# Moving eight folds out of the last unit of a spectral mixing stage, behind a stream of weights

## The chip, the cores and the metric

The kernel runs on one core of one Trainium2 chip. The metric is the device time of one execution in microseconds (us), the median of several runs. The profile is of one execution; its span, from the first to the last instruction, is a little shorter than that execution's time.

## The reference, cut to what matters

```python
# attention with a forgetting gate: q, k, v are (8, 8, 576, 64), f is (8, 8, 576)
log_f = np.log(np.clip(f, 0.0001, 1.0)); cum = np.cumsum(log_f, axis=-1)
scores = scale * q @ k^T + cum[..., :, None] - cum[..., None, :]     # causal
attn_out = softmax(scores) @ v
x = attn_out.transpose(0, 2, 1, 3).reshape(8, 576, 512)

# spectral mixing: w_r, w_i are (64, 512, 512), w_ch is (512, 512), all float32
X = np.fft.rfft(x, axis=1)
Xr, Xi = (np.real(X[:, :n_modes]), np.imag(X[:, :n_modes]))
Yr = np.einsum('bmd,mde->bme', Xr, w_r) - np.einsum('bmd,mde->bme', Xi, w_i)
Yi = np.einsum('bmd,mde->bme', Xr, w_i) + np.einsum('bmd,mde->bme', Xi, w_r)
Y[:, :n_modes] = Yr + 1j * Yi                                         # 64 modes
u = x + np.fft.irfft(Y, n=S, axis=1)
return (u + np.maximum(u @ w_ch, 0.0)).astype(np.float32)             # (8, 576, 512)
```

## The kernel before, in words

The kernel has three stretches. First comes the attention, in 32 steps of two heads each, which leaves x in SBUF (`x_all`, bf16). During it, and after it, the mode weights stream in from memory. Then comes the mixing proper, and last the output stage. The instructions of every engine are issued in the order in which the program is written.

**Units and tiles.** The 64 modes are taken in 16 *units* of 4 modes (`u` from 0 to 15). The weights of a unit come in four *tiles* (`dc` from 0 to 3), each 1 MB in bf16, called (u, dc) here. Tiles with `dc` 0 and 1 hold a quarter of the rows of both `w_r` and `w_i`; tile (u, 2) holds half of the rows of `w_r` and tile (u, 3) the same half of `w_i`. All tiles of `dc` 0 and the first twelve of `dc` 1 are used during the attention. The loop over `u` after it takes the others: tiles 2 and 3 of units 0 to 11, and tiles 1, 2 and 3 of units 12 to 15.

**The stream.** `issue_w` starts the transfer of the next tile in a fixed list (`wseq`), on GpSimd's queue, in one or two DMAs (L156, L165); the last tile, (15, 3), comes in four pieces. Buffers come from a pool of seven (`wpool`), so that a transfer waits for the products of the tile seven before it, and by the semaphores also for the landing of the eighth transfer before it. The call of `issue_w` stands behind the products of each tile.

**The products.** `spec_mms` multiplies a tile with the spectrum of x into a PSUM tile `A` (L194, 8 products of 512 columns). After a unit's last tile, `Yb` is the sum of `A` and what the attention stage had left (VectorE, L744), and four small products with a permutation turn it (L747). The result goes to `YT` for units 0 to 11 (the first 48 modes), and to `YL` for units 12 to 15 (L758). The last unit has its products the other way round (`spec_cols`, L211, 32 products of 16 columns a tile), summed in `accT`.

**The folds.** `xw(b)` computes x times `w_ch` for batch element `b`, in units 2 to 10. A *fold* adds the first 48 modes of one batch element to `x_all` and to that product (`XW`). `fold_modes(b)` turns `YT` (L673) and multiplies it with `w_ch` (L684); ScalarE copies both out of PSUM (L681, L692). `fold` then takes five blocks of rows: the old `x_all` by an identity product (L702), the modes times the inverse basis (L705), a copy back into `x_all` by ScalarE (L706), the modes of the product (L710), and an addition into `XW` by VectorE (L711). This is 8 + 15 = 23 matrix products for each batch element.

Before the change, unit 12 + n takes the folds of batch elements 2n and 2n + 1, ahead of the products of its tiles 1 and 2. So folds 6 and 7 are in unit 15; of fold 7 two blocks of rows stand ahead of the products of tile (15, 2), and three behind them.

**The output stage.** `bases(0)` puts `x_all` and `XW` of the first output block into PSUM (L785); then come the products of tile (15, 3), the last sums into `YL` (L839), the last 16 modes turned (L812) and multiplied with `w_ch` (L823), and for each of 20 blocks the bases, the last modes (L800), a copy by ScalarE (L854), the ReLU and sum by VectorE (L855), and the store (L860, L865).

Of the kernel before, what the change touches and what calls it, by code (L numbers as in the profile page):

```python
# [23 lines left out]
def kernel(  # L24
# [12 lines left out]
    B, H, S, Dh = q.shape  # L37
# [4 lines left out]
    NSB = 5  # L42
    SBLK = [128, 128, 128, 128, 64]
    NEB = D // 128
    BH = B * H
    NPAIR = B * H // 2
    NU = NM // 4
    NF = 12
# [131 lines left out]
    def spec_mms(A, u, dc, first, last):  # L180
        w8 = wtile.pop((u, dc))
        for n in range(2):
            for j in range(4):
                m = 4 * u + j
                st_, sp_ = first and n == 0, last and n == 1
                if dc < 2:
                    M = 32
                    c0 = m * 24 + (8 if n == 0 else 0)
                    lhsT, rhs = XS[:, dc, c0 : c0 + 32], w8[:, n, j, :]
                else:  # L190
                    M = 32 if st_ else 16
                    c0 = 24 * n + (8 if dc == 2 else 0)
                    lhsT, rhs = XPv[:, c0 : c0 + M, m], w8[:, j, n, :]
                nc.tensor.matmul(  # L194
                    A[32 * j : 32 * j + M, :], lhsT=lhsT, rhs=rhs, start=st_, stop=sp_
                )
# [426 lines left out]
    with ExitStack() as bctx:  # L623
# [8 lines left out]
        with ExitStack() as mctx:  # L632
            xtp = mctx.enter_context(tc.tile_pool(name="xtp", bufs=1))
            fsb = mctx.enter_context(tc.tile_pool(name="fsb", bufs=2))
            psA = mctx.enter_context(tc.tile_pool(name="psA", bufs=2, space=PSUM))
            psT = mctx.enter_context(tc.tile_pool(name="psT", bufs=2, space=PSUM))
            psX = mctx.enter_context(tc.tile_pool(name="psX", bufs=4, space=PSUM))

            def xw(b):

                xT = xtp.tile([128, NEB, S], BF16, tag="xT", name="xT")
                for eb in range(NEB):
                    ptr = psT.tile([128, S], BF16, tag="t", name="ptr")
                    for sc in range(NSB):
                        ns = SBLK[sc]
                        nc.tensor.transpose(
                            ptr[:, sc * 128 : sc * 128 + ns],
                            x_all[:ns, eb, b, sc, :],
                            ident_bf[:ns, :ns],
                        )  # L650
                    nc.vector.tensor_copy(xT[:, eb, :], ptr[:, :])  # L651
                if b < 3:
                    XW[b] = xw2.tile([128, NSB, D], BF16, tag="xw", name="XW")
                else:
                    XW[b] = yx[:, b - 3, :].bitcast(BF16).rearrange("p (s e) -> p s e", s=NSB)
                for sb in range(NSB):
                    Ms = SBLK[sb]
                    pxw = psX.tile([128, D], F32, tag="x", name="pxw")
                    for eb in range(NEB):
                        nc.tensor.matmul(  # L660
                            pxw[:Ms, :],
                            lhsT=xT[:, eb, sb * 128 : sb * 128 + Ms],
                            rhs=wch[:, eb, :],
                            start=(eb == 0),
                            stop=(eb == NEB - 1),
                        )
                    nc.scalar.copy(XW[b][:Ms, sb, :], pxw[:Ms, :])  # L667

            def fold_modes(b):

                py = psX.tile([128, D], F32, tag="x", name="py")
                for eb in range(NEB):
                    nc.tensor.matmul(  # L673
                        py[:KF, eb * 128 : (eb + 1) * 128],
                        lhsT=YT[:, eb, b, 0:KF],
                        rhs=ident_bf[:, :],
                        start=True,
                        stop=True,
                    )
                y_sb = fsb.tile([128, D], BF16, tag="ysb", name="y_sb")  # L680
                nc.scalar.copy(y_sb[:KF, :], py[:KF, :])  # L681
                pyw = psX.tile([128, D], F32, tag="x", name="pyw")
                for eb in range(NEB):
                    nc.tensor.matmul(  # L684
                        pyw[:KF, :],
                        lhsT=YT[:, eb, b, 0:KF],
                        rhs=wch[:, eb, :],
                        start=(eb == 0),
                        stop=(eb == NEB - 1),
                    )  # L690
                yw_sb = fsb.tile([128, D], BF16, tag="ywsb", name="yw_sb")
                nc.scalar.copy(yw_sb[:KF, :], pyw[:KF, :])  # L692
                return y_sb, yw_sb

            def fold(b, ys, sbs):

                y_sb, yw_sb = ys
                for sb in sbs:
                    Ms = SBLK[sb]
                    bi = BI[:KF, sb * 128 : sb * 128 + Ms]  # L700
                    pu = psX.tile([128, D], F32, tag="x", name="pu")
                    nc.tensor.matmul(  # L702
                        pu[:Ms, :], lhsT=ident_bf[:Ms, :Ms], rhs=x_all[:Ms, :, b, sb, :], start=True, stop=False
                    )
                    nc.tensor.matmul(pu[:Ms, :], lhsT=bi, rhs=y_sb[:KF, :], start=False, stop=True)  # L705
                    nc.scalar.copy(  # L706
                        x_all[:Ms, :, b, sb, :], pu[:Ms, :].rearrange("p (g c) -> p g c", g=NEB)
                    )
                    pz = psX.tile([128, D], F32, tag="x", name="pz")
                    nc.tensor.matmul(pz[:Ms, :], lhsT=bi, rhs=yw_sb[:KF, :], start=True, stop=True)  # L710
                    nc.vector.tensor_tensor(  # L711
                        XW[b][:Ms, sb, :], pz[:Ms, :], XW[b][:Ms, sb, :], ALU.add
                    )

            xw_plan = {2: 0, 3: 1, 5: 2, 6: 3, 7: 4, 8: 5, 9: 6, 10: 7}
            for u in range(NU):
                last = u == NU - 1
                if not last:
                    A = psA.tile([128, D], F32, tag="a", name="A1")
                first = 2 if u < NX else 1  # L720
                for dc in range(first, NEB - 1 if last else NEB):
                    if dc == NEB - 1 and u in xw_plan:
                        xw(xw_plan[u])
                    split = NSB
                    if u >= NF and dc < 3:
                        b = 2 * (u - NF) + dc - 1
                        split = 2 if b == B - 1 else NSB
                        ys = fold_modes(b)
                        fold(b, ys, range(split))
                    if last:  # L730
                        AT = psA.tile([128, NEB, 8, B], F32, tag="a", name="AT1")
                        spec_cols(AT, dc)
                        nc.vector.tensor_tensor(
                            accT[:], AT[:].rearrange("p e c b -> p e b c"), accT[:], ALU.add
                        )
                    else:
                        spec_mms(A, u, dc, dc == first, dc == NEB - 1)
                    issue_w()
                    if split < NSB:
                        fold(b, ys, range(split, NSB))  # L740
                if last:
                    break
                Yb = ybpool.tile([128, D], BF16, tag="yb", name="Yb")
                nc.vector.tensor_tensor(Yb[:], A[:], yacc[u // 2][:, u % 2, :], ALU.add)  # L744
                yps = psT.tile([128, NEB, 64], F32, tag="t", name="yps")
                for eb in range(NEB):
                    nc.tensor.matmul(  # L747
                        yps[:, eb, :],
                        lhsT=Yb[:, eb * 128 : (eb + 1) * 128],
                        rhs=perm[:],  # L750
                        start=True,
                        stop=True,
                    )
                if u < NF:
                    ydst = YT[:, :, :, 8 * u : 8 * u + 8]
                else:
                    ydst = YL[:, :, :, 8 * (u - NF) : 8 * (u - NF) + 8]
                nc.vector.tensor_copy(  # L758
                    ydst,
                    yps[:].rearrange("p eb (b c) -> p eb b c", b=8),  # L760
                )
# [134 lines left out]
```

## Time and profile before

| what | value |
|---|---|
| median of 3 runs | 442.66 us (439.27 to 443.81) |
| the profiled execution: its own time | 442.7 us |
| the profiled execution: span | 440.7 us |
| mean granted TensorE clock | 0.936 |
| PE busy | 344.5 us, 78% of the span |
| DVE busy | 268.4 us, 61% |
| ACT busy | 233.3 us, 53% |
| GpSimd's DMA queue | 85.64 MB, at 104.9% of 16 engines' span |
| chain that ended last: transfers / PE / DVE | 39% / 34% / 19% |

PE is TensorE's matrix products, PEld its weight loads, DVE VectorE, ACT ScalarE, POOL GpSimd. In a row of the order of time stand the start, the length, the engine, the line, the operation, the tile written and the tiles read, how many, and in brackets the idle time before it with what ended it. A granted clock of 1.00 is TensorE's full clock, and 0.50 half of it.

### The profile page before, as it was taken

How to read it: one execution, taken by the hardware profiler on the slowest of the kernel's cores; microseconds unless marked ns; L12 is line 12 of the kernel's file. 1: busy time of each engine (PE TensorE's matmuls, PEld its weight loads, DVE VectorE, ACT ScalarE, POOL GpSimd, SP SyncE). 2: the span in 40 equal slices, each digit the busy share in tenths (PEclk: the TensorE clock that was granted, in tenths of full speed). 3: DMA queues.
4: the chain of work that ended last, by engine and by line, in shares of the span. 5: the costliest groups of instructions: out<-in, count | busy, mean ns of one | idle time of the engine just before them, and what ended most of it. 6: DMA issues, size and time to landing. Idle time of an engine off the chain costs nothing.

```text
span 440.7 us, 10287 instructions
## 1 busy us (share of the span) xinstructions
PE 344.5 (78%) x4295; PEld 189.9 (43%) x4305; DVE 268.4 (61%) x641; ACT 233.3 (53%) x355; POOL 129.7 (29%) x199
## 2 busy tenths in 40 slices
PE   1678878889889889898893694797885788979993
PEld 0455555555555565555551241343442233325331
DVE  6678888777887778888871221223231356635885
ACT  4567678778787665665640031132222355734673
POOL 6544444453454444444222111012211221100000
PEclk9999999999999999999997598599989699969997
DMA  8999999999999999999999999999999999992698
GB/s 190 205 234 221 230 220 231 232 228 227 231 231 222 231 222 229 221 230 224 232 212 212 212 212 212 212 212 212 211 212 210 211 210 210 210 210 53 219 347 294
DMA packets 68349, 96.75 MB, mean 220 GB/s; under 512 B 3536, under 2 KB 45008, under 8 KB 68304
## 3 DMA queue, kind: packets, MB, share of 16 engines
q0 software_dynamic: 62800, 85.64, 104.9%
q1 hardware_dynamic: 5504, 10.47, 6.8%
q8 instruction: 33, 0.54, 0.4%
q14 instruction: 12, 0.10, 0.1%
HBM read 163.73 MB, written 9.44 MB: 393 GB/s over the span
## 4 chain that ended last, share of the span: by engine, by line
DMA 39%; PE 34%; DVE 19%; ACT 3%; issue 3%; POOL 1%; DVEq 0%; POOLq 0%; ACTq 0%
DMA w<-in_moe_w_i_dram 22%; DMA w<-in_moe_w_r_dram 15%; DVE vT L384 5%; DVE x_all L492 4%; DVE qkT L360 4%; PE pav L477 4%; PE A L194 4%; PE sps L432 3%; PE tv L382 3%; PE pd L521 3%; PE vp L393 2%; PE U L785 2%; DMA qk<-in_k_dram 2%; PE Z L785 2%; DVE vn L372 2%
## 5 line engine op out<-in xcount | busy, mean ns | idle before, releaser
L439 ACT ACTIVATE et<-sps 128x1024 bf16<-128x1024 f32 x96 | 96.0, 1050 | 12.6 <-PE sps L432 10.2
L744 DVE TENSOR_TENSOR Yb<-A,yx 128x512 bf16<-128x512 f32 x15 | 10.4, 692 | 67.6 <-PE A L194 67.6
L477 PE MATMUL pav<-vs,et 128*128 128x65 bf16 (+1 forms) x896 | 51.2, 197 | 0.2 <-DVE vn L372 0.2
L360 DVE COPY qkT<-tp 128x640 bf16<-128x640 bf16 x64 | 48.8, 763 | 3.1 <-PE tp L355 3.0
L477 PEld LDWEIGHTS <-et 128*128 128x128 bf16 (+1 forms) x896 | 36.5, 102 | 17.2 <-issue 13.3
L194 PE MATMUL A<-w,XP 128*16 128x512 bf16 (+1 forms) x240 | 22.6, 457 | 27.1 <-DMA w<-in_moe_w_i_dram 15.6
L660 PE MATMUL pxw<-wch,xT 128*128 128x512 bf16 (+1 forms) x152 | 39.1, 403 | 1.0 <-DVE xT L651 0.4
L432 PE MATMUL sps<-qkT 64*128 64x512 bf16 (+4 forms) x320 | 38.9, 306 | 1.1 <-DVE qkT L360 1.1
L492 DVE TENSOR_TENSOR x_all<-pav,rcp 128x384 bf16<-128x384 f32 (+2 forms) x96 | 36.2, 377 | 3.3
L355 PE MATMUL tp<-ident_bf,qk 128*64 128x128 bf16 x576 | 29.3, 231 | 9.9 <-DMA qk<-in_k_dram 9.9
L384 DVE COPY vT<-tv 128x576 bf16<-128x576 bf16 x32 | 24.2, 757 | 19.3 <-PE tv L382 19.3
L667 ACT CAST XW<-pxw 128x512 bf16<-128x512 f32 (+1 forms) x15 | 8.8, 585 | 48.3 <-PE pxw L660 48.3
L165 POOL DMA_DIRECT2D w<-in_moe_w_r_dram x16 | 11.9, 743 | 70.1 <-PE A L194 56.7
L404 ACT COPY vs<-vp 128x576 bf16<-128x576 bf16 x32 | 20.5, 640 | 21.4 <-PE vp L400 21.4
L156 POOL DMA_DIRECT2D w<-in_moe_w_r_dram x27 | 20.5, 759 | 38.5 <-PE A L194 8.6
L667 ACT CAST yx<-pxw 128x512 bf16<-128x512 f32 (+1 forms) x25 | 14.6, 585 | 32.4 <-PE pxw L660 32.4
L165 POOL DMA_DIRECT2D w<-in_moe_w_i_dram x19 | 13.3, 700 | 55.8 <-PE A L194 26.1
L109 POOL DMA_DIRECT2D qk<-in_q_dram x32 | 19.7, 614 | 33.8 <-PE tp L355 7.8
L706 ACT CAST x_all<-pu 128x512 bf16<-128x512 f32 (+1 forms) x40 | 23.4, 584 | 9.0 <-PE pu L705 8.0
L491 DVE RECIPROCAL rcp<-pav 128x6 f32<-128x6 f32 (+2 forms) x96 | 16.2, 169 | 16.3 <-PE pav L477 16.1
L156 POOL DMA_DIRECT2D w<-in_moe_w_i_dram x27 | 20.4, 756 | 17.5 <-DMA w<-in_moe_w_i_dram 8.2
L109 POOL DMA_DIRECT2D qk<-in_k_dram x32 | 19.4, 605 | 20.2 <-DMA w<-in_moe_w_r_dram 6.5
(134 smaller groups left out, 666.5 us busy)
## 6 DMA issues: line engine op xcount, KB each, us to landing
w<-in_moe_w_r_dram POOLq DMA_DIRECT2D x16, 1024.0 KB, 29.6
w<-in_moe_w_i_dram POOLq DMA_DIRECT2D x15, 1024.0 KB, 32.1
w<-in_moe_w_r_dram POOLq DMA_DIRECT2D x27, 512.0 KB, 11.1
w<-in_moe_w_i_dram POOLq DMA_DIRECT2D x27, 512.0 KB, 12.5
vt<-in_v_dram POOLq DMA_DIRECT2D x29, 288.0 KB, 10.6
out_dram<-o_sb SPq DMA_DIRECT2D x16, 512.0 KB, 3.4
qk<-in_q_dram POOLq DMA_DIRECT2D x32, 144.0 KB, 10.7
qk<-in_k_dram POOLq DMA_DIRECT2D x32, 144.0 KB, 10.8
```

The costliest lines, as they stand in the source:

```text
L109: nc.gpsimd.dma_start(qk[64 * n : 64 * n + 64, :, :], src[b, 2 * g : 2 * g + 2, :, :].rearrange("h (p r) d -> p h (r d)", p=64),)
L156: nc.gpsimd.dma_start(w8[:, t, :, :], src[4 * u : 4 * u + 4, dc * 128 : (dc + 1) * 128, :].rearrange("m p e -> p m e"),)
L165: nc.gpsimd.dma_start(w8[:, j : j + step, :, :].rearrange("p m r e -> p m (r e)"), src[m : m + step, 256:512, :].rearrange("m (p r) e -> p ...
L194: nc.tensor.matmul(A[32 * j : 32 * j + M, :], lhsT=lhsT, rhs=rhs, start=st_, stop=sp_)
L355: nc.tensor.transpose(tp[64 * hp : 64 * hp + 64, r - r0, :, :].rearrange("p n c -> p (n c)"), qk[:, hp, r * 64 : r * 64 + 64], ident_bf[:, :],
L360: nc.vector.tensor_copy(st[i]["T"][:].rearrange("p n (c r) -> p n c r", r=9)[:, :, :, r0:r1], tp[:, 0 : r1 - r0, :, :].rearrange("p r n c ...
L384: nc.vector.tensor_copy(st[i]["vT"][:].rearrange("p (c r) -> p c r", r=9), tv[:].rearrange("p r c -> p c r"))
L432: nc.tensor.matmul(ps[:, hp, c : c + n], lhsT=KT[sl, jb * 128 : jb * 128 + 128], rhs=QT[sl, i0 : i0 + n], start=True, stop=True,)
L439: nc.scalar.activation(st[i]["et"][:, T, :, :], ps[:], ACT.Exp, scale=scale)
L477: nc.tensor.matmul(pav[:Ms, sb % 3, hp, :], lhsT=eblk(i, hp, jb, sb), rhs=rhs, start=(jb == 0), stop=(jb == sb),)
L492: nc.vector.tensor_tensor(x_all[:ns, g, b, lo:hi, :].rearrange("p s (h d) -> p s h d", h=2), pav[:ns, lo % 3 : lo % 3 + n, :, 0:Dh], _stri ...
L660: nc.tensor.matmul(pxw[:Ms, :], lhsT=xT[:, eb, sb * 128 : sb * 128 + Ms], rhs=wch[:, eb, :], start=(eb == 0), stop=(eb == NEB - 1),)
```

## The change

The eight folds are taken in units 12 to 14, three to a unit, in the order of the batch elements. The first two of a unit stand ahead of the products of its tiles 1 and 2, as before. The third stands behind the products of its tile 3, after the sum into `Yb` and ahead of the four small products with the permutation. Unit 14 takes only two, ahead of its tiles 1 and 2, and the last unit none. A fold is no longer split.

```diff
-            def fold(b, ys, sbs):
+            def fold(b, ys):
 
                 y_sb, yw_sb = ys
-                for sb in sbs:
+                for sb in range(NSB):
...
             xw_plan = {2: 0, 3: 1, 5: 2, 6: 3, 7: 4, 8: 5, 9: 6, 10: 7}
+            steps = [(u, dc) for u in range(NF, NU - 1) for dc in range(1, NEB)]
+            fold_plan = dict(zip(steps, range(B)))
             for u in range(NU):
...
-                    split = NSB
-                    if u >= NF and dc < 3:
-                        b = 2 * (u - NF) + dc - 1
-                        split = 2 if b == B - 1 else NSB
-                        ys = fold_modes(b)
-                        fold(b, ys, range(split))
+                    if dc < NEB - 1 and (u, dc) in fold_plan:
+                        b = fold_plan[u, dc]
+                        fold(b, fold_modes(b))
                     if last:
...
                     issue_w()
-                    if split < NSB:
-                        fold(b, ys, range(split, NSB))
                 if last:
                     break
                 Yb = ybpool.tile([128, D], BF16, tag="yb", name="Yb")
                 nc.vector.tensor_tensor(Yb[:], A[:], yacc[u // 2][:, u % 2, :], ALU.add)
+                if (u, NEB - 1) in fold_plan:
+                    b = fold_plan[u, NEB - 1]
+                    fold(b, fold_modes(b))
                 yps = psT.tile([128, NEB, 64], F32, tag="t", name="yps")
```

Here NF is 12, NU 16, NEB 4, NSB 5 and B 8.

## The prediction

> **What bounds the kernel now.** I read the page's rows of forty slices first, then the chain of work that ended last from 300 us on, then the order of time of TensorE and of GpSimd's transfers from 325 us on, and last the clock and the transfers in steps of one microsecond around 400 us.
>
> ```profile
> PEclk9999999999999999999997598599989699969997
> DMA  8999999999999999999999999999999999992698
> ```
>
> Each digit is a fortieth of the span (11.0 us). The transfers are busy from the start to slice 36, so the weights set the time up to about 400 us. Only after that do other engines decide.
>
> ```profile
> 359.39 28.41 DMA w<-in_moe_w_i_dram
> 387.84 1.09 PE A L194 x7
> ...
> 400.65 0.91 PE AT L211 x32
> 402.86 0.33 PE pu L702
> 403.19 0.33 PE pu L705
> 403.85 0.69 DVE yx L711
> 404.59 0.39 PE Z L785
> 405.03 1.09 PE AT L211 x32
> ```
>
> Columns: start, length, what. The last wait of the chain for a weight ends at 387.84 us. From there TensorE is never free: fold of batch 6, tile (15,1), fold of batch 7 around tile (15,2), the first output block's bases (L785), and only at 405.03 us the 32 products of the last tile (15,3). All of the output stage hangs on these: VectorE takes them up at 406.14.
>
> ```profile
> 373.36 0.54 POOL L165 DMA_DIRECT2D w<-in_moe_w_i_dram  x1 [4.18 <-DMA w<-in_moe_w_i_dram]
> 383.18 0.53 POOL L165 DMA_DIRECT2D w<-in_moe_w_i_dram  x1 [4.40 <-DMA w<-in_moe_w_r_dram]
> ```
> ```profile
> DMA to landing us min/median/max: 19.7/19.7/19.7
> ```
>
> The last tile comes in four pieces. The first is issued at 373.36, the fourth at 383.18, and the fourth takes 19.7 us to land: **402.9 us**. The queue moves nothing after 402.75. So the last products start 2.1 us after their weights are there, because of folds that needed no late weight at all.
>
> ```profile
> 387.00:388.00 1.00, 0.16 (x4) 0.16 (x7) 0.00 (x0) 0.00 (x0) 0.00 (x0) 0.80 1.21 210
> 394.00:395.00 1.00, 1.00 (x5) 0.37 (x4) 0.49 (x2) 0.55 (x1) 0.00 (x0) 0.79 1.14 213
> 401.00:402.00 1.00, 1.00 (x23) 0.69 (x20) 0.85 (x2) 0.05 (x1) 0.00 (x0) 1.00 0.16 29
> ```
>
> Columns: stretch, its length, busy time of TensorE, of its weight load, of VectorE, ScalarE and GpSimd, then the granted clock, the DMA share and GB/s. The clock fell to half within 387 to 388 us (0.80, so at about 387.4), after TensorE had waited from 385.91 to 387.84, and came back at about 394.4. The last unit's folds then keep TensorE busy, and the output stage begins at full clock.
>
> **The change, part by part.** No operation is added or taken away; the 8 folds of 23 matrix products each only move.
>
> ```profile
> 360.43 0.40 PE L673 MATMUL py<-ident_bf,YT 128*96 128x128 bf16 x4
> ...
> 365.57 0.61 PE L194 MATMUL A<-w,XS 128*32 128x512 bf16 x8
> ```
>
> One fold at full clock is 365.57 - 360.43 = 5.14 us of TensorE; a weight tile's 8 products take 0.54. At half clock (345.73 to 352.80, and 389.9 to 396.81) a fold takes 7.
>
> *Units 12 to 14.* Starting where before starts (fold 0 at 345.73, weights as before): fold 0 to 352.80, tile (12,1) to 353.34, fold 1 to 358.44, tiles (12,2) and (12,3) to 359.52. All this is unchanged. Now fold 2 follows at once, to 364.66, the four small products of L747 to 364.8, fold 3 to 369.9, (13,1) to 370.5, fold 4 to 375.6, (13,2) and (13,3) to 376.7, fold 5 and L747 to 382.0, fold 6 to 387.1, (14,1) to 387.6, fold 7 to 392.8, (14,2) and (14,3) to 393.9. No weight is late for it: the waits of before, 0.95 us for (13,3) at 372.86 and 1.93 us for (14,3) at 387.84, are now covered by folds, and with them the half clock that made fold 6 take 6.9 us. L747's four products wait behind the third fold; only the copy into YL waits for them, and YL is read in the output stage.
>
> *The transfers.* GpSimd's order of transfers is unchanged. A tile is issued when the products of the tile seven before it are done and when the eighth transfer before it has landed. Tile (15,2) waits for (13,1): 370.5 and a little instead of an issue at 368.44, some 2.7 us later. The first pieces of (15,3) wait for (13,2): about 377 instead of 373.36. The fourth waits for a landing at about 382.7, as before. I cost this at nothing: at 371 us the tiles (13,3), (14,1), (14,2), (14,3) and (15,1) are outstanding, 5 MB at 4.9 us per MB (212 GB/s), so 24 us of work covers it. Without that cover it would cost up to 2.7 us.
>
> *The last unit.* After 393.9: sum into Yb and L747 to 394.9 (0.8 us of waiting, as at 388.95), (15,1) landed near 392.7 (363.26 + 29.4), its 32 products to 395.8; then TensorE waits for (15,2), which lands at 368.44 + 29.4 = 397.85. Its products, the accumulation (0.42 us) and the four bases of block 0 fit before the last piece. At full clock the last 8 products then run from 402.9 and end near 403.25, where before they ended at 406.12: **2.87 us gained**.
>
> *The clock.* This is what the moved work did besides: it kept TensorE busy. Now there are waits of 0.8 and of 395.8 to 397.85, 2.05 us. The wait of 1.93 us was enough for a fall to half, and so were 0.80 and 1.06 us close together (316 to 318; the clock fell near 319.4); 0.95 and 0.80 us (372 to 374) were not. So I expect half clock from about 397.6. How long? From the first products after such a wait to the return it took 6.65 us (278.55 on), 4.6 (318.17), 7.1 (342.88) and 6.3 (387.84). Counted from 397.85 that is 402.5 to 405.0, on average 404.1. At half clock from 397.85 on, a product of 512 columns takes 0.43 instead of 0.216 us. No row shows the 128x16 products of L211 at half; between 1.4 times (the transposes of L646, 2.06 to 2.89) and 2 times I take 2, as they too wait on weight loads. Then (15,2) 1.8, accumulation 0.6, bases 1.7, two pieces 0.9, the third 0.45: TensorE is at the fourth piece at 403.3, and through it at 403.75, 0.5 us late. If the clock is back at 402.5 about 0.1 is lost, if at 405.0 another 0.45 in L812: 0.1 to 0.95. I take 0.8, nearer the upper end, because the short waits (0.37 us at L812, 0.5 at L800) break the run of busy time. Nothing later makes it up: from 409 us TensorE is busy without a gap, 6.18 us for nine tiles, where VectorE needs 9 x 0.65 = 5.9.
>
> *Sum.* 442.7 (span 440.7 and 2.0 around it, the median of the runs being 442.66) - 2.87 + 0.8 = **440.6 us**, for this case 439.9 to 441.4.
>
> [...]
>
> **The rivals.**
> *1. The clock stays full.* Then the whole 2.87 us is kept: 439.8. For it speaks that waits of 0.8 and 0.95 us left it full; against it, that 1.93 us did not. [...]
> *2. Slower: the half clock holds into the output stage.* Between 397.85 and 402.9 TensorE is only partly busy, so the stretch may count anew from 402.9. At half from there: last products 0.6, wait 0.37, L812 0.63, L823 1.9, L800 0.6, wait 0.3, L800 0.6, so at 402.9 + 5.0 it stands where full clock stands after 3.3: 1.7 us lost, and 0.5 more for each further microsecond. With 4.6 to 7.1 us that is 1.6 to 2.75 lost, 441.4 to 442.6. It decides the sign from 402.9 + 7.3 = 410.2 on. From 273.62, where another wait came between, the clock was back only after 11.6 us; that long it loses 1.7 + 3.3 = 5.0 and gives 444.8. For it: the waits at L812 and L800 come right there. Against: from 403.3 on TensorE is nearly full, as in the short returns.
> *3. The weights land later.* If the later issue of (15,2) came through, the last landing is 2.7 us later and the time 443.3. For it: the issue really moves. Against: 24 us are queued.
> *4. The folds don't fit.* Should the clock be half through folds 2 to 7, each costs 1.8 us more, 10.8 in all, and TensorE ends them near 404.7 instead of 393.9, after the landing. The three last tiles and the bases take 4.0 more, to 408.7, and the time is 442.7 + 408.7 - 406.12 = 445.3. Against it: no wait is left there.
>
> **How the numbers follow.** Forecast 0.52; full clock 0.17; half clock into the output stage 0.22 (0.14 below 442.7, 0.08 above it); late weights 0.05; folds 0.04. The three runs of before reach from 439.27 to 443.81, so a median may lie a microsecond beside any case. The range of 438.7 to 443.6 leaves out the upper part of rival 2, rival 4, and the low edge of rival 1. A measurement tells about 1% from no change, 438.2 and 447.1 here. Faster by more needs rival 1 and a run to run shift: 0.08. Slower by more needs rival 2 beyond its longest row: 0.04. Within 1%: 0.88.
>
> **What would show it.** Right: folds without a gap from 345.7 to about 393; the last products of L211 within a microsecond of the fourth piece's landing near 402.9; half clock for some microseconds from about 397 to 405; L839 near 403.8 instead of 406.14; the output stage otherwise as long as before (34.6 us from L839 to the end). Wrong: a landing after 404, a clock that stays 1.0 around 400, or one at 0.5 beyond 410.

## The result: slower by 0.3%

The changed kernel takes 443.22 us (median of 22 runs, 441.75 to 444.44), the kernel before 441.72 us (22 runs beside them, 439.27 to 443.81). The ratio is 1.0032, with a 95% interval of 1.0019 to 1.0044. The forecast was 440.6 us, 2.1 less than the 442.7 it started from. The time lies within the range of 438.7 to 443.6, but it moved the other way.

### The profile page after: what moved, and what is told of

The parts are those of the page before. It is cut to its first block, busy times and chain, and to the rows that moved or that the text cites. A ratio compares the mean times of both kernels' runs of the same rounds, so it can differ in the third digit from the quotient of the medians.

```text
span 440.6 us, 10296 instructions
## 1 busy us (share of the span) xinstructions
PE 351.1 (80%) x4305; PEld 192.4 (44%) x4305; DVE 268.4 (61%) x641; ACT 233.0 (53%) x355; POOL 129.3 (29%) x199
## 4 chain that ended last, share of the span: by engine, by line
DMA 45%; PE 29%; DVE 16%; issue 4%; ACT 3%; POOL 1%; DVEq 0%; POOLq 0%
DMA w<-in_moe_w_i_dram 29%; DMA w<-in_moe_w_r_dram 15%; DVE vT L384 4%; PE pav L477 4%; DVE x_all L492 4%; DVE qkT L360 4%; PE A L194 3%; PE sps L432 3%; PE tv L382 3%; PE vp L393 2%; PE U L785 2%; DMA qk<-in_k_dram 2%; PE pd L521 2%; PE Z L785 2%; DVE vn L372 2%
## 5 line engine op out<-in xcount | busy, mean ns | idle before, releaser
L439 ACT ACTIVATE et<-sps 128x1024 bf16<-128x1024 f32 x96 | 96.0, 1049 | 13.7 <-PE sps L432 10.6
L477 PE MATMUL pav<-vs,et 128*128 128x65 bf16 (+1 forms) x896 | 52.4, 199 | 0.2 <-DVE vn L372 0.2
L477 PEld LDWEIGHTS <-et 128*128 128x128 bf16 (+1 forms) x896 | 37.4, 103 | 18.0 <-issue 13.5
L660 PE MATMUL pxw<-wch,xT 128*128 128x512 bf16 (+1 forms) x160 | 41.1, 412 | 0.0
L432 PE MATMUL sps<-qkT 64*128 64x512 bf16 (+4 forms) x320 | 40.0, 314 | 1.1 <-DVE qkT L360 1.1
L194 PE MATMUL A<-w,XP 128*16 128x512 bf16 (+1 forms) x240 | 21.1, 441 | 21.8 <-DMA w<-in_moe_w_i_dram 12.2
L855 DVE SCALAR_TENSOR_TENSOR o_sb<-Z,u_sb 128x512 f32<-128x512 f32 x36 | 23.0, 685 | 4.9 <-ACT u_sb L854 3.9
```

Of the source, the lines that this page charges most:

```text
L194: nc.tensor.matmul(A[32 * j : 32 * j + M, :], lhsT=lhsT, rhs=rhs, start=st_, stop=sp_)
L432: nc.tensor.matmul(ps[:, hp, c : c + n], lhsT=KT[sl, jb * 128 : jb * 128 + 128], rhs=QT[sl, i0 : i0 + n], start=True, stop=True,)
L439: nc.scalar.activation(st[i]["et"][:, T, :, :], ps[:], ACT.Exp, scale=scale)
L477: nc.tensor.matmul(pav[:Ms, sb % 3, hp, :], lhsT=eblk(i, hp, jb, sb), rhs=rhs, start=(jb == 0), stop=(jb == sb),)
L660: nc.tensor.matmul(pxw[:Ms, :], lhsT=xT[:, eb, sb * 128 : sb * 128 + Ms], rhs=wch[:, eb, :], start=(eb == 0), stop=(eb == NEB - 1),)
```

## The profile after

The profiled execution of the changed kernel took 443.14 us, with a span of 440.6. The page's rows of forty slices differ from those of before most in slices 36 to 38 (385.5 to 418.6 us): the 6 of slice 36 has become a 9, as the fall of the clock at 387.6 us is gone, and the 9s of slices 37 and 38 have become 5 and 8:

```profile
PEclk9999999999999999999998597599979699995898
DMA  8999999999999999999999999999999999992698
```

The chain of work that ended last (start, length, what) now hangs on the weights up to the last piece, as forecast:

```profile
382.82 19.71 DMA w<-in_moe_w_i_dram
402.53 0.05 issue
402.58 0.42 PE AT L211 x8
403.00 0.02 issue
403.02 0.30 DVE YL L839
403.33 0.05 issue
403.37 0.61 PE pyl L812 x4
403.98 1.87 PE pywl L823 x5
...
407.29 0.96 PE U L785 x2
408.26 0.85 PE Z L785 x2
```

The fourth piece lands at 402.53, its products follow at once, and L839 starts at 403.02, 3.1 us before the 406.14 of before. Then come the new prices. Two products of L785 take 0.96 us instead of 0.54, and the eight of L823 take 1.92 in the order of time (first row) where before they took 1.05 (second row):

```profile
403.91 1.92 PE L823 MATMUL pywl<-wch,YL 128*64 128x512 bf16 x8
406.82 1.05 PE L823 MATMUL pywl<-wch,YL 128*64 128x512 bf16 x8
```

The order of time of the last unit shows the waits that led to this:

```profile
392.18 1.07 PE L194 MATMUL A<-w,XP 128*16 128x512 bf16 x16
394.05 0.29 PE L747 MATMUL yps<-perm,Yb 128*128 128x64 bf16 x4 [0.80 <-DVE Yb L741]
394.18 0.95 PE L211 MATMUL AT<-XS,w 128*128 128x16 bf16 x32
397.57 1.10 PE L211 MATMUL AT<-XP,w 128*128 128x16 bf16 x32 [2.44 <-DMA w<-in_moe_w_r_dram]
399.19 1.01 PE L785 MATMUL U<-x_all,ident_bf 128*128 128x512 bf16 x2 [0.52 <-DVE accT L732]
402.58 0.41 PE L211 MATMUL AT<-XP,w 128*128 128x16 bf16 x8 [0.82 <-DMA w<-in_moe_w_i_dram]
```

The clock answers. In this trace it is at half for 6.83 us (342.54 to 349.37), at full for 47.79, and at half again for 13.64 (397.16 to 410.80): 2, 14 and 4 times 3.41 us. So here is the same execution in stretches of 3.41 us, laid so that the clock's changes at 397.16 and 410.80 fall on their ends (stretch, length, busy time of TensorE, of its weight load, of VectorE, ScalarE and GpSimd, then granted clock, DMA share and GB/s):

```profile
393.75:397.16 3.41, 1.08 (x36) 0.98 (x36) 1.10 (x3) 0.00 (x0) 0.00 (x0) 1.00 1.06 199
397.16:400.57 3.41, 2.48 (x36) 1.57 (x37) 0.42 (x1) 0.00 (x0) 0.00 (x0) 0.50 0.66 125
400.57:403.98 3.41, 2.21 (x40) 1.52 (x40) 0.49 (x2) 0.00 (x0) 0.00 (x0) 0.50 0.14 26
403.98:407.39 3.41, 3.09 (x13) 0.80 (x14) 0.72 (x2) 1.58 (x3) 0.00 (x0) 0.50 0.00 0
407.39:410.80 3.41, 3.41 (x11) 0.84 (x10) 1.76 (x3) 1.16 (x3) 0.00 (x0) 0.50 0.36 135
410.80:414.20 3.40, 3.40 (x25) 1.17 (x24) 2.80 (x6) 2.41 (x5) 0.00 (x0) 1.00 0.47 171
```

After a stretch with 1.08 us of busy time the clock is at half. It stays there for four whole stretches and comes back at 410.80, behind the first one in which TensorE was busy throughout. So the first 7.8 us behind the start of L839 run at half clock.

Two intervals tell most of the story, in this profile and in all that follow. The first is from the issue of the fourth piece to L839: how soon the last products are done, measured against the stream of weights, which itself comes up to a microsecond earlier or later in nine of the ten profiles. The second is from L839 to the start of the last products (L800): how fast TensorE gets through the output stage. (In kernels with added code the same lines have other numbers; the text keeps these.) These are the rows, the first two of before, the last of the changed kernel, whose L839 stands in the chain above:

```profile
406.14 0.49 DVE L839 TENSOR_TENSOR YL<-AT,accT 128x128 bf16<-128x128 f32 x2 [1.61 <-PE AT L211]
433.31 0.40 PE L800 MATMUL Z<-yl,BI 32*64 32x512 bf16 x2
433.05 0.40 PE L800 MATMUL Z<-yl,BI 32*64 32x512 bf16 x2
```

The kernel before: 406.14 - 383.18 = 22.96 us, and 433.31 - 406.14 = 27.17 us. The changed kernel: 403.02 - 382.82 = 20.20, and 433.05 - 403.02 = 30.03. It gains 2.76 and loses 2.86.

That explains why these two profiled spans are equal (440.7 and 440.6), but not yet why the medians differ by 1.5 us.

## The experiments

Theory A: the folds of the last unit kept TensorE's clock up. Without them it falls to half, and the output stage pays. Theory B: the move costs something by itself, through later transfers or the earlier place of the folds. Rival C, for the kernel before: its time is set by the last landing, and its own folds don't matter.

### The waits filled

```diff
+            def fill(n):
+                pf = psX.tile([128, D], F32, tag="x", name="pf")
+                for _ in range(n):
+                    nc.tensor.matmul(pf[:], lhsT=ident_bf[:, :], rhs=wch[:, 0, :], start=True, stop=True)
...
+                        if dc == 2:
+                            fill(10)
                         spec_cols(AT, dc)
...
                 if last:
+                    fill(2)
                     break
...
+                if u == NU - 2:
+                    fill(3)
...
+        def fill2(j):
+            for _ in range((0, 0, 4, 3)[j]):
+                nc.tensor.matmul(pyw0[:], lhsT=ident_bf[:, :], rhs=wch[:, 0, :], start=True, stop=True)
+
+        spec_cols(AT, NEB - 1, fill2)
```

`spec_cols` now calls `fill2` ahead of each of the four pieces of tile (15, 3).

> The changed kernel, with 22 products of 512 columns whose results nobody reads added in TensorE's waits of unit 14's end and of the last unit: 3 behind unit 14's sum, 10 ahead of tile (15,2), 2 behind it, and 4 and 3 between the last tile's pieces. Theory A (TensorE's waits in the last unit put its clock at half, and the output stage begins at half clock, which loses the 3.1 us that the earlier last products had gained): the granted clock stays 1.00 from about 350 us to the end of the products, L839 starts near 403.0 as in the changed kernel, the stretch from L839 to the end is 34.6 us as before and not 37.6, and the time is some 3 us under the changed kernel's 443.2, about 440.2. Theory B (the move itself costs, by later transfers or by the order of the folds, and the clock only goes along): the time stays at 443 or rises by the added work, however the clock stands.

Measured: 439.69 us (12 runs, 439.32 to 441.21), ratio to before 0.9963 (0.9942 to 0.9984). The windows of this kernel's profile:

```profile
394.00:397.00 3.00, 3.00 (x46) 1.79 (x46) 0.85 (x2) 0.00 (x0) 0.00 (x0) 1.00 1.06 198
397.00:400.00 3.00, 2.12 (x38) 1.41 (x38) 0.42 (x1) 0.00 (x0) 0.00 (x0) 1.00 0.63 117
400.00:403.00 3.00, 2.83 (x40) 1.47 (x38) 0.00 (x0) 0.00 (x0) 0.00 (x0) 1.00 0.23 43
403.00:406.00 3.00, 2.08 (x24) 0.89 (x20) 1.18 (x3) 1.24 (x3) 0.00 (x0) 1.00 0.00 0
```

The clock is 1.00 throughout. L839 starts 20.20 us behind the fourth piece's issue, as in the changed kernel, and the output stage takes TensorE 27.18 us, as in the kernel before (27.17). Added work made the changed kernel faster: its ratio to the runs of before beside it goes from 1.0032 to 0.9963, some 3 us. Theory A holds, and B falls: the folds stand where the change put them, and the order of the transfers is the changed kernel's.

### One fold taken back

```diff
-            fold_plan = dict(zip(steps, range(B)))
+            fold_plan = dict(zip(steps, range(B - 1)))
+            fold_plan[NU - 1, 2] = B - 1
```

> The changed kernel with one fold taken back: fold 7 stands in the last unit, between the products of tiles (15,1) and (15,2). Theory A: TensorE waits some 3 us for (15,1) at about 389.6 to 392.6 and its clock falls there, but fold 7 then keeps it busy from 392.6 on without a gap, so that the clock is back by about 400 and full when the last piece lands; L839 starts between 403.0 and 404.2, the stretch behind it is 34.6 us, and the time is about 440 to 441. Theory B (what costs is the folds' earlier place in units 12 to 14): as seven of eight folds are still early, the time stays within half a microsecond of 443.2.

Measured: 441.74 us (12 runs, 440.16 to 444.43), ratio 1.0000 (0.9977 to 1.0024). I had expected 440 to 441, and the profiled run (442.64) shows why it failed. The clock did come back, at about 396.6. It fell again where I had not looked:

```profile
397.00:400.00 3.00, 3.00 (x21) 1.18 (x20) 2.77 (x5) 2.47 (x5) 0.00 (x0) 1.00 0.68 125
400.00:403.00 3.00, 2.43 (x61) 1.92 (x58) 1.03 (x2) 0.21 (x1) 0.00 (x0) 1.00 0.25 48
403.00:404.00 1.00, 0.61 (x14) 0.50 (x10) 0.49 (x2) 0.00 (x0) 0.00 (x0) 0.74 0.00 0
404.00:407.00 3.00, 2.68 (x15) 0.67 (x13) 0.69 (x1) 0.90 (x2) 0.00 (x0) 0.50 0.00 0
```

From 400 to 403 TensorE counts as busy for 2.43 of 3 us, yet the clock falls near 403.5. The output stage then took 29.64 us. This is one of the longer of the 12 runs; whether the clock fell in the shorter ones was not seen. What fills those 3 us is mostly the products of 16 columns of L211. This gave the next question.

### Short products instead of long ones

The filled kernel again, each product of 512 columns replaced by eight of 16 columns (`pf[:, 0:16]`, `rhs=wch[:, 0, 0:16]`).

> The first filled kernel with its 22 added products of 512 columns replaced by 176 of 16 columns, each with its own weight load: the same places and about the same time, as 32 such products of L211 take 0.91 us. It asks what keeps the clock up. In the second kernel the clock fell near 403.2 though TensorE's records show it busy for all but some 0.6 us of the 3.4 us before. Theory A1 (what counts is how much of the array's time carries columns, and short products count little): the clock falls near 397 as in the changed kernel, the output stage begins at half clock, and the time is 442.5 to 443.5. Theory A2 (any stream of instructions without a long wait counts): full clock, 439.7 as with the long products.

Measured: 445.17 us (5 runs, 444.10 to 446.58), ratio 1.0088 (1.0060 to 1.0116), slower than the changed kernel too. Its windows:

```profile
392.00:396.00 4.00, 3.89 (x134) 3.31 (x127) 2.15 (x4) 0.22 (x1) 0.00 (x0) 1.00 1.12 210
393.16:396.57 3.41, 3.30 (x131) 3.21 (x127) 1.26 (x3) 0.00 (x0) 0.00 (x0) 1.00 1.12 212
396.00:397.00 1.00, 0.70 (x29) 0.60 (x25) 0.00 (x0) 0.00 (x0) 0.00 (x0) 0.79 0.94 180
397.00:400.00 3.00, 1.77 (x49) 1.60 (x50) 0.42 (x1) 0.00 (x0) 0.00 (x0) 0.50 0.67 124
```

TensorE is busy for 3.89 of the 4 us ahead of 396, from about 392.8 on with almost nothing but short products. The stretch of 3.41 us that ends at 396.57 has 3.30 us busy (second row), and there the clock falls as it did behind 1.08 us in the changed kernel. Theory A2 falls: 3.30 us of busy time in the records did not keep the clock up. The run goes with A1, but what A1 counts was not measured by itself. The time went beyond A1's 443.5, because the last products came later as well (L839 at 21.72 us behind the fourth piece's issue, 1.5 more than in the changed kernel), ahead of an output stage of 30.73.

### Only the first waits filled

The filled kernel without the products at the last unit's end and between the pieces; 13 of 22 are left.

> The changed kernel with only the first 13 added products: 3 behind unit 14's sum and 10 ahead of tile (15,2). The waits behind that, 0.5 us for the accumulation and 0.8 us for the last piece, stay. Theory A1 (every stretch of 3.4 us is judged by itself, and the last one before 402.6 holds two waits and mostly short products): no fall near 397, but one between 400 and 404, with half clock to 407 or 410, so the output stage loses nearly as much, and the time is 442 to 443. Rival (the 2.4 us wait for tile (15,2) alone takes the clock down): full clock through the output stage, 439.7 to 440.2.

Measured: 443.61 us (11 runs, 441.97 to 447.22), ratio 1.0036 (1.0014 to 1.0058). The profiled run is the longest of them; its weights came 3 us later than usual (fourth piece issued at 385.95), and all times shift with them. The median is above the 442 to 443 that I expected.

```profile
400.00:401.00 1.00, 0.30 (x11) 0.30 (x12) 0.00 (x0) 0.00 (x0) 0.00 (x0) 1.00 0.78 150
401.00:402.00 1.00, 0.78 (x28) 0.69 (x25) 0.18 (x1) 0.00 (x0) 0.00 (x0) 1.00 0.47 84
402.00:403.00 1.00, 0.70 (x3) 0.30 (x3) 0.25 (x1) 0.00 (x0) 0.00 (x0) 0.75 0.27 49
```

No fall during the filled wait; one at 402.5, after waits of 0.76 and 0.52 us with short products between. Half clock then lasts to about 416.2 (expected: 407 or 410, so later even without those 3 us), and the output stage takes 31.00 us. The 2.4 us wait is not the cause by itself: filling it alone moved the fall and saved nothing (443.61 us). The rival falls. The fall lies where theory A1 put it, between 400 and 404, but that every stretch is judged by itself stays a theory: what the trace shows is a fall and a return 13.7 us apart, 4 times 3.41.

### The kernel before, filled and looked at again

```diff
+                        if (u, dc) == (NU - 2, NEB - 1):
+                            fill(8)
                         spec_mms(A, u, dc, dc == first, dc == NEB - 1)
...
+                if u == NU - 2:
+                    fill(3)
```

> The kernel before, with 8 products that nobody reads ahead of tile (14,3), where TensorE waited 1.93 us, and 3 behind unit 14's sum. It asks how much the clock's fall at 387.4 costs the kernel before. Theory A: the clock stays full there, fold 6 takes 5.1 us instead of 6.9, the last products start near 403.3 instead of 405.0, and the time falls to the lower half of the runs of before, about 440.7, with fewer runs above 442. Rival C (the time of before is set by the last landing at 402.9 and not by the folds): no change, 441.7.

Measured: 440.39 us (12 runs, 439.59 to 441.77), ratio 0.9971 (0.9950 to 0.9992), and no run above 442, where 11 of the 29 runs of before beside it lie. The clock stays at 1.00, L839 comes 20.69 us behind the fourth piece's issue, and the output stage takes 27.16. Rival C falls.

> The kernel before once more, for another profile. If its runs differ by whether the clock falls near 387 us, a profile of a run near 440.7 shows full clock through folds 6 and 7, and one near 442.6 shows half clock in fold 6, as the first profile did. If the runs differ for another reason, the clock rows do not go with the time.

Measured: 441.13 us (one run). Its clock fell at about 373.7 and was back at 377; through folds 6 and 7 it is full:

```profile
387.00:388.00 1.00, 0.65 (x8) 0.17 (x7) 0.14 (x1) 0.00 (x0) 0.00 (x0) 1.00 1.17 205
394.00:395.00 1.00, 1.00 (x37) 1.00 (x35) 0.82 (x2) 0.33 (x1) 0.00 (x0) 1.00 1.10 207
402.00:403.00 1.00, 0.95 (x33) 0.92 (x31) 0.00 (x0) 0.00 (x0) 0.00 (x0) 1.00 0.00 0
```

L839 is 20.69 us behind the fourth piece's issue, not 22.96, and the output stage takes 27.17. In such a run the last products end only half a microsecond after the changed kernel's, and there is next to nothing to gain.

> The kernel before, a third profile, for where its clock falls. If the clock falls near 387 us: L839 near 406, time 442.5. If it does not: L839 near 403.2, time 441 or less.

Measured: 441.79 us (one run). The clock fell at about 387.6, as in the first profile; L839 23.13 us behind the fourth piece's issue, output stage 27.16. So the same kernel does both. The time was 0.7 us under what I expected, as the weights came 0.7 us earlier.

What parts the second profile from the third, as far as two profiles can show it, is where the stretches of 3.41 us lie, counted from each profile's own changes of the clock (373.62 in the second; 387.6 in the third, which is four stretches behind 373.95). Ahead of fold 4 TensorE does the same at the same times in both: tile (13,3) at 372.18 and L747 at 373.62, behind waits of 0.7 to 0.8 us each. But the ends of the stretches lie 0.33 us apart. The second profile's stretch, and its wait for tile (14,3):

```profile
370.21:373.62 3.41, 1.85 (x19) 0.60 (x19) 1.92 (x3) 0.73 (x2) 0.54 (x1) 1.00 1.19 208
387.17 0.65 PE L194 MATMUL A<-w,XP 128*16 128x512 bf16 x8 [0.73 <-DMA w<-in_moe_w_i_dram]
```

The same in the third:

```profile
370.54:373.95 3.41, 1.91 (x26) 0.79 (x25) 1.65 (x4) 0.58 (x1) 0.54 (x1) 1.00 1.20 209
387.17 0.73 PE L194 MATMUL A<-w,XP 128*16 128x512 bf16 x8 [1.95 <-DMA w<-in_moe_w_i_dram]
```

In the second the clock fell at 373.62. Fold 4 then took 6.3 us instead of 5.1, TensorE came later to tile (14,3), waited 0.73 us for it instead of 1.95, and the clock stayed full through folds 6 and 7. In the third it stayed full at 373.95, and it fell at 387.6, behind the longer wait. By the two intervals the early fall cost nothing (20.69 and 27.17 us): a wait for weights absorbed it. That the place of the stretches decided is my reading, not shown.

> The changed kernel once more, for another profile. Theory A: whatever the moment at which the clock is judged, its waits from 393.3 to 397.6 are long enough for a fall between 396 and 400, and half clock reaches to 404 at least, mostly to 407 to 411; L839 near 403, time 442 to 444.

Measured: 442.92 us (one run). The clock fell at 397.2 and was back at about 410.8; the intervals are 20.21 and 29.87 us. The changed kernel's loss is nearly the same in both of its profiles. Their clocks also fell in the same place (397.16 and 397.19), so what another place would cost was not seen.

### All profiles together

| kernel | fourth piece's issue to L839 | L839 to last L800 | clock |
|---|---|---|---|
| before, first profile | 22.96 | 27.17 | half 387.6 to 394.4 |
| before, third | 23.13 | 27.16 | half 387.6 to 394.4 |
| before, second | 20.69 | 27.17 | full from 377 |
| before, filled | 20.69 | 27.16 | full from 348.5 |
| changed, first profile | 20.20 | 30.03 | half 397.2 to 410.8 |
| changed, again | 20.21 | 29.87 | half 397.2 to 410.8 |
| fold 7 taken back | 20.41 | 29.64 | half 393.2 to 396.6 and 403.5 to 410.3 |
| filled with short products | 21.72 | 30.73 | half 396.6 to 413.6 |
| first waits only | 20.24 | 31.00 | half 402.5 to 416.2 |
| changed, filled | 20.20 | 27.18 | full from 350 |

Against a run of before with full clock the change costs 30.03 - 27.17 - (20.69 - 20.20) = 2.4 us, against one with half clock in fold 6 it costs 0.1. The measured 1.5 lies between. How many runs of before are of either kind was not counted: three profiles are too few.

The intervals leave out a third part, from the last L800 to the end of the span. It is 7.0 to 8.7 us in the ten profiles, 7.4 and 7.6 in the two first. In the second profile of before it is 8.7 and in the third 7.0, so that their times lie only 0.7 us apart where their two intervals together lie 2.4 apart. Why it varies was not looked into.

## Why the prediction was wrong, point by point

**The move in units 12 to 14 was right.** Folds without a gap: the products of (14,2) and (14,3) begin at 392.18 and end by 393.3 (forecast: 393.9). No weight was late in these units. Tile (15,2) was issued at 370.29 instead of 368.44 and was taken up at 397.57 (397.85), and the last piece landed at 402.53 (402.9). Rivals 3 and 4 fall with that. The last products ended at 403.0 against 403.25 to 403.75.

**The fall of the clock was right, its length was not.** This is the step that failed: "Counted from 397.85 that is 402.5 to 405.0, on average 404.1". The clock was back at 410.8, and the 0.8 us that I charged for it was 2.86, all of it behind the last products. That alone uses up the gain: between the two first profiles 2.76 us were gained and 2.86 lost. I had counted from the first products after the wait, as if any work brought the clock back. In the four rows that I took it from, the stretch of 3.41 us that ends at the return has 3.19, 3.20, 3.41 and 3.41 us busy. Here the waits of 0.52, 0.82, 0.39 and 0.32 us and the short products came first, and behind three stretches with 2.48, 2.21 and 3.09 us busy the clock was still at half. That is rival 2, which had the right place, a turn of the sign at 410.2, and nearly the right price: 1.7 us and 0.5 for each further microsecond make some 3.1 us for a return at 410.8. I gave it 0.22.

**The gain was measured against one execution.** The "2.87 us gained" was real beside the first profile (2.76, measured from the fourth piece's issue), but that profile held a fall near 387.5 which not every run has. The second profile of before leaves 0.49 of it. I had seen that fall, and had used it as a property of the kernel. Against that run even my own 0.8 us would have made a loss of 0.3. The starting time was too high as well: the 442.66 us were the median of three runs, and 22 runs have 441.72.

**Sizes that did no harm.** I took twice the time for L211's short products at half clock. In the changed kernel's last unit a row of 32 is 1.10 us long (397.57), where at full clock it was 0.96 to 1.07 in the kernel before, and TensorE waited 0.82 us for the last piece instead of coming 0.5 late to it. The 7 us for a fold at half clock are a mix: the clock was back at 350.0 and at 394.4, within both of the folds that I read it from. Rival 4's price rests on it, and no run shows a fold wholly at half clock. One of the four lengths of half clock is 6.6 us by the return at 394.4, not 6.3; the average of 404.1 agrees with 6.6.

**Rival 1 fell.** The longest gap in the last unit was 2.44 us, ahead of the products at 397.57, and the clock was at half from 397.16 on.

## What to carry to other kernels

Work that is taken out of a wait may have been holding TensorE's clock up: before moving it, write down what TensorE does ahead of the next dense stage, in steps of 3.41 us, as the clock's changes lay whole multiples of that apart here, and don't count on products of 16 columns: 3.30 us busy of 3.41, almost all with them, did not hold the clock here. If a dense stage follows a wait for transfers, fill the wait, with real work or with products that nobody reads; here that made both placements of the folds faster, 0.9963 (0.9942 to 0.9984) and 0.9971 (0.9950 to 0.9992) of before. And look for what may differ between executions, above all a clock change, before a wait in a single profile is taken as a gain to be had.

## What the runs showed of the hardware

Busy instructions alone did not hold the clock up. With 3.30 of 3.41 us busy, almost all in products of 16 columns, it fell at 396.6; with products of 512 columns in the same places it stayed at 1.00. Two shapes alone were tested, and that the columns carried are what decides was not shown.

In the table half clock lasts 3.4, 6.8, 13.6 to 13.7 or 17.0 us: 1, 2, 4 or 5 times 3.41.

In busy time the return took more than the stay. Stretches with 2.48, 2.21 and 3.09 us busy of 3.41 did not bring the clock back in the changed kernel. In the first profile of the kernel before 1.73 us (384.18 to 387.59) took it down, while 2.02 us did not:

```profile
370.53:373.94 3.41, 2.02 (x19) 0.60 (x18) 1.79 (x4) 0.91 (x2) 0.54 (x1) 1.00 1.21 208
373.94:377.35 3.41, 2.76 (x19) 1.49 (x20) 1.25 (x3) 1.73 (x4) 0.54 (x1) 1.00 1.16 210
```

A part of this may be that a busy microsecond at half clock carried half the columns: in fold 6 of that profile two products of 512 columns start 0.43 us apart at half clock (392.04 and 392.47), and 0.22 us apart behind the return (394.53 and 394.75). Nor does busy time alone tell the return: in the changed kernel's profile the stretch from 318.65 to 322.06 has 3.41 us busy, and the clock stayed at half, while in the kernel before the one from 319.32 to 322.74 has 3.20 and the clock came back. What exactly is counted stays open.
